# A recurrent attention kernel and its mixing layer: channel tiles in pairs, token weights by hardware loads, another state transpose, a new order

## The chip, the core and the metric

The kernel runs on one core of a Trainium2 chip. The core has five engines with a queue each: TensorE (PE, with its weight loads shown apart as PEld), VectorE (DVE), ScalarE (ACT), GpSimd (POOL) and SyncE (SP). Here SP computes nothing; it issues DMAs. Matrix products go to PSUM, the other data lie in SBUF. The metric is the device time of one execution in microseconds (us). The profile shows one execution; its span runs from the first to the last instruction.

## What is computed

The input has 4 batches, 8 heads, 768 tokens and head width 40, all in fp32. A recurrence over tokens gives `y`, one 40 x 40 state per batch and head, and a mixing layer follows, in which the heads of a token are laid side by side (320 channels):

```python
y[:, :, t] = einsum('bhd,bhde->bhe', r_t, state)
Sa = einsum('bhde,bhe->bhd', state, a_t)
state = state * w_t[:, :, None, :] - einsum('bhd,bhe->bhde', Sa, b_t) + einsum('bhd,bhe->bhde', v_t, k_t)

x = y.transpose(0, 2, 1, 3).reshape(B, S, H * D)
theta = x @ w_theta
yr = einsum('ts,bsd->btd', w_tok_r, x * cos(theta))
yi = einsum('ts,bsd->btd', w_tok_i, x * sin(theta))
u = x + yr + yi
out = u + maximum(u @ w_ch, 0)
```

## The kernel before

The tokens are cut into 24 tiles of 128 (six per batch, numbered 0 to 23 throughout). Within a tile the recurrence is solved with masked matrix products, and the state is carried from tile to tile. The whole program is one list, the string ORDER (L19 to L133). Each entry names a step, a tile, sometimes the engine (A, V and G for ACT, DVE and POOL, S for a DMA transpose issued by SP) and sometimes a PSUM bank (@0 to @3). A loop at L800 calls one function per entry, and `keep` holds the order on every engine. So the place of an entry among those of its own engine is its place in the queue, and a step that waits holds up everything behind it on its engine.

The steps, in the order in which one tile passes through them:

- LDW, LDK, LDB, LDA, LDR, LDV load w, k, b, a, r, v. LDW and LDR load two tiles at once. They go through SP, in four cases at the start through ACT's queue (the letter A).
- LN takes the logarithm of w for two tiles. CSI and CSE are running sums of it by products with triangular masks. INVW and WI are their exponentials. CSE (L384) also makes the sums over a whole tile.
- KH and AH scale k, b and a. TRK and TRA transpose them on PE (eight and four transposes of 128x128), EKBT and EAT copy the results out of PSUM. CV and CR cast v and r, TRV and TRR transpose them, EVT and ERT copy.
- PSI, PHI, LV and LU are score products, eight each, with copies EPSI, EPHI, ELV, ELU. A copy on DVE also masks; a copy on ACT is masked afterwards on POOL (MPSI, MPHI, MLV, MLU).
- X0 and NU (copies ENX, ENU) solve the tile; NUT (copy ENUT) transposes the result. GT makes the new state. The old state is added by a product with the identity (GI) or by an add on DVE (EGA), and EGT scales. GD transposes the state, EGD copies it. Y makes the tile's output, EX scales it into x.
- XT, EXT, TH, ETH and SIN make theta and its sines. ZR multiplies them with x on POOL. LDT loads a row block of a token-weight matrix, WT transposes it, EWT copies it. YR, six entries per tile of two products each, mixes the tokens. EU adds x, UT and EUT transpose u, CH multiplies with w_ch in three products, EO makes the output and ST stores it. LDC loads w_theta and w_ch.

A tile of x or u has 320 channels. It is kept as 384 columns with 64 zeros (`x_t`, `u_t`, L216 and L217), so that transposes (`tr_three`, L646) and products (`mix3`, L660) are three whole ones of 128.

```python
u_t = padded("u", [128, 3 * 128], 3, lambda t: t[:, DM:])
...
wrows[tb, n] = tile_of(wrow, [128, S], BF16, f"wtok_row_{n}")
keep(nc.gpsimd.dma_start(out=wrows[tb, n],
                         in_=moe_w_tok[n][tb * 128:(tb + 1) * 128, :]))
...
tr_one(i, b, "gdps", gt_t[i % 2].rearrange("p g c d -> p (g c) d"))
```

The second piece (L721) is LDT: POOL issues a DMA that turns fp32 into bf16, into one of three buffers per matrix. The third (L615) is GD: four transposes of 128x128 for eight heads of width 40 padded to 64, whose result is bf16.

Of the kernel before, what the change touches and what calls it, by code (L numbers as in the profile page):

```python
# [19 lines left out]
LDW:0 LDK:0A LDB:0 LDA:0A LDA:1 LDB:1A LDK:1 LDV:0A LN:0A LDC:0.0G LDT:0.0G CSI:0@0 LDC:0.1G CSE:0@1 WI:0A  # L20
INVW:0A KH:0V TRK:0@0 AH:0V EKBT:0A TRA:0@3 LDW:2 EAT:0V LDR:0 KH:1V PHI:0@1 PSI:0@0
EPSI:0A MPSI:0G CV:0A LDB:2 EPHI:0A AH:1V TRK:1@1 EKBT:1V LN:2A TRA:1@2 MPHI:0G LDV:1 TRV:0@3
LDK:2 X0:0@0 EAT:1V CSI:2@0 CR:0A ENX:0V LDA:2 PSI:1@1 INVW:2A EVT:0V NU:0 ENU:0A EPSI:1V
TRR:0@1 PHI:1@0 LDB:3 ERT:0A GT:0@2 CV:1A LDK:3 CSE:2@1 EPHI:1V TRV:1@3 ERT:1A NUT:0@0 KH:2G
WI:2A EGT:0V LV:0@0 LDA:3 EVT:1V X0:1@1 ENX:1A ENUT:0A ELV:0V LDV:2 AH:2G GD:0@2 LDR:2 TRK:2@3
KH:3G LV:1@1 NU:1 EKBT:2A LU:0@0 ELV:1V LDW:4 TRA:2@0 ENU:1A LDV:3 ELU:0A NUT:1@3 AH:3G EAT:2V
GT:1@1 ENUT:1V PSI:2@1 TRK:3@0 EGD:0V EPSI:2V LDK:4 LDA:4 GI:1 EKBT:3A CV:2G TRA:3@3 LU:1@0
ELU:1A CR:2G PHI:2@1 EGT:1V X0:2@2 EAT:3V EPHI:2V MLU:0G ENX:2A LN:4A LDB:4 TRR:2@0 PSI:3@0
LDR:4 CV:3G PHI:3@1 MLU:1G Y:0@1 EPSI:3A MPSI:3G EPHI:3V NU:2 TRV:2@3 CSE:4@0 LDV:4 ENU:2A
ERT:2A EVT:2V GT:2@2 EX:0V WI:4A AH:4G CSI:4@1 INVW:4A Y:1@3 LDW:6 NUT:2@1 EGA:2V EGT:2V ERT:3A  # L30
ENUT:2V LV:2@0 LDA:5 TRV:3@2 EX:1V X0:3@1 ELV:2A KH:4G EVT:3V LU:2@1 ENX:3V ELU:2V LV:3@0
TRA:4@0 ELV:3A LDK:5 NU:3 TRK:4@3 LDB:5 GD:1@2 EAT:4V ENU:3A MLV:2G XT:0@0 EKBT:4V CR:4A GT:3@1
GI:3 EGD:1V EGT:3V PSI:4@1 EPSI:4V CV:4G PHI:4@0 LN:6A TRR:4@3 EPHI:4A NUT:3@2 MLV:3G Y:2@1
ENUT:3V LDB:6 LDA:6 AH:5G LDK:6 CSI:6@1 X0:4@2 EX:2V EXT:0A ERT:4A INVW:6A TRV:4@0 ENX:4V
MPHI:4G LDV:5 KH:5G LU:3@0 ERT:5A XT:1@1 NU:4 ELU:3V EXT:1A CSE:6@1 LDV:6 LDT:1.1G ENU:4A
TRA:5@3 WI:6A NUT:4@1 EVT:4V ENUT:4A TRK:5@2 LDK:7 EAT:5V AH:6G XT:2@0 EKBT:5V LV:4@0 TH:0@3
ELV:4V KH:6G PSI:5@1 GD:2@1 LDR:6 SIN:0A TH:1@2 LU:4@0 CV:5G GT:4@3 GI:4 EXT:2A EPSI:5V CV:6G
ZR:0G LDW:8 TRA:6@0 PHI:5@1 LDB:7 ELU:4A LDA:7 EGD:2V EGT:4V TH:2@1 SIN:1A EAT:6V MLU:4G SIN:2A
TRK:6@3 X0:5@0 GD:3@2 EPHI:5V EKBT:6V ENX:5A LDB:8 Y:3@1 ZR:1G EGD:3V EX:3V PSI:6@0 EPSI:6V
TRV:5@3 TRV:6@2 Y:4@1 LN:8A LDK:8 NU:5 PHI:6@1 EVT:6V ENU:5V EVT:5A CR:6G X0:6@2 EPHI:6V  # L40
LDT:1.0G KH:7G TRR:6@0 ENX:6A CSI:8@0 INVW:8A LDA:8 LDV:7 EX:4V NUT:5@3 LV:5@1 ELV:5A LDB:9
ERT:6V AH:7G ENUT:5V TRK:7@1 CSE:8@0 ERT:7V KH:8G TRA:7@3 WI:8A LDV:8 LV:6@1 EAT:7V EKBT:7V
ELV:6A LU:5@0 LDA:9 GD:4@0 NU:6 ELU:5V AH:8G PSI:7@1 TRK:8@3 LDK:9 ENU:6A EGD:4A CV:7A MLV:5G
# [93 lines left out]
def kernel(  # L137
# [247 lines left out]
    def cse(i, b):  # L385
# [448 lines left out]
```

## Time and profile before

| | |
|---|---|
| median of 3 runs | 207.87 us (206.63 to 208.0) |
| the profiled execution | 206.92 us |
| its span | 205.2 us |
| TensorE clock granted, mean | 0.999 |
| DMA | 34.17 MB, mean 167 GB/s |
| chain that ended last | PE 80%, ACT 6%, DVE 5% |

A profile row of instructions gives the line, the engine, the operation, output and inputs by name with their shapes, the count, then busy time and the mean duration in ns. The line is often that of a helper: L270 and L272 are the copies, L275 the multiplication, L278 the product, L282 the transpose. So the names of the tiles tell the steps apart. `sm` and `sc` are small and large PSUM banks. A timeline row gives start and duration in us, and in square brackets how long the engine sat idle before it and on what. Rows marked SPq or ACTq are the DMA issues of a queue.

### The profile page before, as it was taken

To read this page: it belongs to the slowest core of one execution; us is meant where nothing else is said; L and a number is where in the kernel's file an instruction comes from. 1 tells how busy PE (TensorE), PEld (TensorE's weight loads), DVE (VectorE), ACT (ScalarE), POOL (GpSimd) and SP (SyncE) were. 2 spreads that over 40 slices of the span, in tenths; PEclk is the share of its full clock that TensorE was granted. 3 is DMA by queue.
4 is the path that set the end of the run, shared out by engine and by line. 5 is a ranking of instruction groups with operands and counts; after the bars stand their busy time and mean duration, and the time that the engine had idled before them with its cause. 6 is when DMAs were issued, how large, how long until landed. Compare 5 with 4: busy or idle time off the path is not lost.

```text
span 205.2 us, 7809 instructions
## 1 busy us (share of the span) xinstructions
PE 190.1 (93%) x3266; PEld 147.5 (72%) x3266; DVE 170.6 (83%) x334; ACT 154.3 (75%) x259; POOL 147.1 (72%) x157
## 2 busy tenths in 40 slices
PE   0389999999999999999999999999999999999992
PEld 0166777877777887887887877887877787777671
DVE  7256899999999997999799998989888797975653
ACT  2367799997989997999899788987898685822100
POOL 8225778899989699998966886993989785634000
PEclk9999999999999999999999999999999999999999
DMA  7999999998898999899489989987979996433342
GB/s 136 187 240 159 225 171 178 173 230 140 153 221 154 213 159 216 164 213 226 103 171 193 192 172 238 192 135 161 169 97 154 218 129 140 99 90 103 102 150 96
DMA packets 144802, 34.17 MB, mean 167 GB/s; under 512 B 139520, under 2 KB 144768, under 8 KB 144768
## 3 DMA queue, kind: packets, MB, share of 16 engines
q1 hardware_dynamic: 138176, 30.26, 76.5%
q0 software_dynamic: 2432, 2.77, 8.4%
q10 hardware_dynamic: 4160, 0.66, 2.2%
q8 instruction: 25, 0.41, 0.9%
q14 instruction: 9, 0.07, 0.1%
HBM read 29.13 MB, written 3.93 MB: 161 GB/s over the span
## 4 chain that ended last, share of the span: by engine, by line
PE 80%; ACT 6%; DVE 5%; issue 2%; ACTq 2%; POOL 2%; POOLq 0%; DVEq 0%
PE sm L278 39%; PE sc L278 22%; PE sm L282 20%; ACTq L331 1%; ACT kbT L270 1%; ACT psi L270 1%; DVE phi L275 1%; ACTq L326 1%; ACT Wi_two L412 1%; ACT lw_two L338 1%; POOL z L275 1%; DVE lamu L275 1%; DVE rvT L272 1%; POOL lamv L554 1%; POOL phi L554 1%
## 5 line engine op out<-in xcount | busy, mean ns | idle before, releaser
L275 POOL TENSOR_TENSOR kb<-raw_kb,invW_two 128x640 bf16<-128x640 f32 x22 | 33.9, 1542 | 5.5 <-ACT invW_two L373 3.6
L275 POOL TENSOR_TENSOR z<-cs,x 128x640 bf16<-128x640 f32 x22 | 30.8, 1403 | 5.3 <-ACT cs L677 5.3
L278 PE MATMUL sm<-z,wtok_r 128*128 128x320 bf16 x120 | 34.3, 299 | 0.0
L278 PE MATMUL sm<-z,wtok_i 128*128 128x320 bf16 x120 | 34.2, 299 | 0.0
L275 POOL TENSOR_TENSOR ah<-raw_a,Wi_two 128x320 bf16<-128x320 f32 x22 | 19.0, 866 | 8.5 <-issue 5.2
L275 DVE TENSOR_TENSOR psi<-sc,mask_p 128x1024 bf16<-128x1024 f32 x16 | 19.5, 1219 | 1.0 <-PE sc L278 0.9
L554 POOL TENSOR_SCALAR_AFFINE_SELECT psi<-psi 128x1024 bf16<-128x1024 bf16 x8 | 8.7, 1093 | 14.0 <-ACT psi L270 11.6
L275 DVE TENSOR_TENSOR phi<-sc,mask_p 128x1024 bf16<-128x1024 f32 x14 | 17.1, 1219 | 1.6 <-PE sc L278 1.4
L278 PE MATMUL sc<-aT,kbT 64*128 64x128 bf16 x384 | 17.3, 225 | 1.1 <-ACT kbT L270 0.7
L275 DVE TENSOR_TENSOR lamu<-sc,mask_p 128x1024 bf16<-128x1024 f32 x14 | 17.1, 1220 | 0.6 <-PE sc L278 0.3
L282 PE MATMUL sm<-ident,kb 128*128 128x128 bf16 x184 | 14.9, 227 | 2.6 <-DVE kb L275 2.3
L278 PEld LDWEIGHTS <-wtok_r 128*128 128x128 bf16 x144 | 14.0, 97 | 4.6 <-issue 0.3
L270 ACT COPY rvT<-sm 128x512 bf16<-128x512 bf16 x28 | 15.9, 593 | 1.3 <-PE sm L282 0.7
L278 PEld LDWEIGHTS <-wtok_i 128*128 128x128 bf16 x144 | 14.1, 98 | 3.9 <-issue 0.2
L275 DVE TENSOR_TENSOR lamv<-sc,mask_p 128x1024 bf16<-128x1024 f32 x13 | 15.9, 1220 | 1.0 <-PE sc L278 0.5
L677 ACT ACTIVATE cs<-sm 128x320 f32<-128x320 f32 x26 | 9.9, 452 | 8.5 <-PE sm L278 8.4
L278 PEld LDWEIGHTS <-kbT 64*128 64x128 bf16 x384 | 11.9, 97 | 5.8 <-issue 2.4
L278 PEld LDWEIGHTS <-rvT 64*128 64x128 bf16 (+1 forms) x272 | 13.6, 95 | 2.9 <-issue 0.5
L278 PE MATMUL sm<-kb,lamv 128*128 128x40 bf16 x192 | 15.0, 180 | 0.0
L278 PE MATMUL sm<-kb,lamu 128*128 128x40 bf16 x192 | 14.9, 179 | 0.0
L282 PEld LDWEIGHTS <-kb 128*128 128x128 bf16 x184 | 11.5, 101 | 4.2 <-DVE kb L275 2.3
L554 POOL TENSOR_SCALAR_AFFINE_SELECT lamu<-lamu 128x1024 bf16<-128x1024 bf16 x10 | 10.9, 1090 | 4.1 <-ACT lamu L270 4.1
(137 smaller groups left out, 625.0 us busy)
## 6 DMA issues: line engine op xcount, KB each, us to landing
raw_w_two<-in_w_dram SPq DMA_DIRECT2D x12, 320.0 KB, 4.8
raw_r_two<-in_r_dram SPq DMA_DIRECT2D x12, 320.0 KB, 4.8
out_dram<-oo SPq DMA_DIRECT2D x24, 160.0 KB, 2.5
raw_kb<-in_b_dram SPq DMA_DIRECT2D x23, 160.0 KB, 4.6
raw_a<-in_a_dram SPq DMA_DIRECT2D x23, 160.0 KB, 4.5
raw_kb<-in_k_dram SPq DMA_DIRECT2D x23, 160.0 KB, 4.3
raw_v<-in_v_dram SPq DMA_DIRECT2D x23, 160.0 KB, 4.7
wtok_row<-in_moe_w_tok_r_dram POOLq DMA_DIRECT2D x6, 192.0 KB, 4.8
```

The source lines that it names most:

```text
L270: keep(nc.scalar.copy(out=out, in_=in_))
L272: keep(eng[e].tensor_copy(out=out, in_=in_))
L275: keep(eng[e].tensor_tensor(out=out, in0=in0, in1=in1, op=ALU.mult))
L278: keep(nc.tensor.matmul(out, lhsT=lhsT, rhs=rhs, start=start, stop=stop, skip_group_check=True))
L282: keep(nc.tensor.transpose(out=out, in_=in_, identity=ident))
L326: keep(queue[e].dma_start(out=tiles[i].raw_kb[:, j], in_=source(ap, i)))
L331: keep(queue[e].dma_start(out=t, in_=source(ap, i)))
L338: keep(nc.scalar.activation(out=q.lw[:, :, :, 0:D], in_=q.raw_w.rearrange("p h (j d) -> p j h d", j=2), func=AF.Ln))
L412: keep(nc.scalar.activation(out=two, in_=q.cse[:, LO:LO + 2 * DM + 16], func=AF.Exp))
L554: keep(nc.gpsimd.affine_select(out=flat, in_=flat, compare_op=ALU.is_ge, fill=0.0, base=-1, pattern=[[0, 2 * G], [1, 128]], channel_multip ...
L677: keep(nc.scalar.activation(out=cs[i % 5][:, c], in_=tiles[i].theta, func=AF.Sin, bias=(math.pi / 2, 0.0)[c]))
```

## The change

u is kept in pairs of tiles without padding: two tiles side by side are 640 columns, five blocks of 128. The even tile transposes the first two blocks, the odd one the other three. The block in the middle holds the last 64 channels of the even tile and the first 64 of the odd one. The new step CHR multiplies it with two copies of rows of w_ch, each with one half of zeros, for both tiles. So CH takes two products, and CHR one for each of its two tiles. The even tile's output then waits for the odd tile. A step THR would do the same for x, but the new order doesn't use it. w_ch needs four loads in place of two.

The token weights are loaded as fp32 by SP (LDT), into one buffer per matrix, and cast to bf16 by a new step CW, into one buffer per matrix. GD is four products of the state with 80 of the 128 columns of an identity, with a result in fp32. The sums over a tile are a step of their own (CST). No load goes through ACT's queue. The buffers for theta are three, not four. The order is new throughout. Its entries, where the counts differ:

| step | before | after |
|---|---|---|
| GD, GI, EGA | 15, 5, 11 | 16, 9, 7 |
| XT, UT, WT, NUT, TRV | 19, 14, 11, 20, 22 | 16, 16, 12, 22, 23 |
| CH, CHR | 24, 0 | 24, 12 |
| LDT on POOL, on SP | 12, 0 | 0, 12 |
| CW on POOL, on ACT | 0, 0 | 9, 3 |
| LDC | 4 | 6 |
| EGD on DVE, ACT, SP | 7, 8, 5 | 3, 13, 4 |
| EKBT on DVE, ACT | 16, 7 | 20, 3 |
| ENX and ENU on DVE, ACT | 24, 24 | 16, 32 |
| EAT, ERT, EVT, ENUT together on DVE, ACT, SP | 48, 42, 6 | 53, 40, 3 |
| copies of scores on DVE, ACT | 57, 39 | 57, 39 |
| EXT on DVE, ACT, SP | 12, 7, 5 | 11, 5, 8 |
| EUT on DVE, ACT, SP | 6, 8, 10 | 4, 12, 8 |

The diff, cut to its core, with the first and last lines of the order and those around the first token weights:

```diff
-LDW:0 LDK:0A LDB:0 LDA:0A LDA:1 LDB:1A LDK:1 LDV:0A LN:0A LDC:0.0G LDT:0.0G CSI:0@0 LDC:0.1G CSE:0@1 WI:0A
-INVW:0A KH:0V TRK:0@0 AH:0V EKBT:0A TRA:0@3 LDW:2 EAT:0V LDR:0 KH:1V PHI:0@1 PSI:0@0
...
-YR:23.3 YR:23.4 YR:23.5 EU:22V UT:22@1 CH:21@0 EU:23V EUT:22A EO:21V UT:23@3 CH:22@2 EUT:23V
-CH:23@1 EO:22V ST:21 EO:23V ST:22 ST:23
+LDW:2 LDW:0 LDK:0 LDA:1 LDC:0.0G LDC:0.2G LDA:0 LN:0A LDB:0 CSE:0@0 CSI:0@1 LN:2A CST:0 LDB:1
+LDK:1 INVW:0A WI:0A LDK:2 AH:0V CSI:2@1 CSE:2@0 AH:1V KH:0V CST:2 LDB:2 TRA:0@0 TRK:0@3 LDV:0
+EAT:0A INVW:2A LDR:0 EKBT:0V LDA:2 WI:2A KH:1V PHI:0@1 EPHI:0A PSI:0@0 LDV:1 KH:2G TRA:1@2
...
+MPSI:1G GT:0@0 CV:1A EAT:2V EGT:0V ERT:0A NUT:0@2 LDR:2 PSI:2@0 ENUT:0A PHI:2@1 EPSI:2A TRV:1@3
...
+GT:7@0 AH:9G LN:10A TH:3@3 CV:8G LDK:10 EKBT:9V TH:4@1 ELU:7V GI:7 CW:0.0G PHI:8@0 SIN:3A EVT:7V
+LDT:1.0 MLU:6G EGT:7V LV:7@1 SIN:4A TRA:9@2 XT:5@3 EXT:5A X0:8@0 EPHI:8V LDB:10 WT:0.0@1 EAT:9V
+CW:0.1G ENX:8A EWT:0.0A ELV:7V TH:5@3 MLV:6G PSI:9@0 EPSI:9V SIN:5A WT:0.1@2 CR:8G NU:8 TRV:8@1
+EVT:8V LDT:1.1 ENU:8A LDA:10 Y:7@3 EWT:0.1A CV:9G CSI:10@1 EX:7V PHI:9@0 GT:8@0 LDR:10 ZR:5G
+CW:1.0G NUT:8@2 GI:8 LDV:10 EPHI:9V TRR:8@1 EGT:8V Y:6@3 INVW:10A CSE:10@0 KH:10G LDB:11 CST:10
...
+YR:22.5 YR:21.3 EO:19V ST:19 EU:22V YR:21.4 YR:23.0@0 YR:21.5 EU:21V YR:23.1 YR:23.2 YR:23.3
+UT:21@3 YR:23.4 YR:23.5 EU:23V EUT:21A UT:22@1 CH:20@2 EUT:22A CHR:21@3 CH:21 EO:20V UT:23@0
+CH:22@1 EUT:23V ST:20 EO:21V ST:21 CHR:23@2 EO:22V CH:23 ST:22 EO:23V ST:23
...
+    u_two = [consts.tile([128, 2 * DM], BF16, name=f"u_two_{n}") for n in range(3 if twin_u else 0)]
+    def home(i, twins, one, two):
+        if i not in twins:
+            t = one[i % len(one)]
+            return t[:, 0:DM], t
+        t = two[i // 2 % len(two)]
+        if i % 2:
+            return t[:, DM:2 * DM], t[:, 256:2 * DM]
+        return t[:, 0:DM], t[:, 0:256]
...
-    wrow = ctx.enter_context(tc.tile_pool(name="wrow", bufs=3))
+    wraw = ctx.enter_context(tc.tile_pool(name="wraw", bufs=1))
+    wrow = ctx.enter_context(tc.tile_pool(name="wrow", bufs=1))
...
-        tr_one(i, b, "gdps", gt_t[i % 2].rearrange("p g c d -> p (g c) d"))
+        tiles[i].gdps = bank(b)
+        some = ident.rearrange("p (c d) -> p c d", c=2)[:, :, 0:D]
+        for g in range(G):
+            mm(tiles[i].gdps[:, g * 80:g * 80 + 80],
+               gt_t[i % 2][:, g].rearrange("p c d -> p (c d)"), some, True, True)
...
+        elif i % 2 == 0:
+            setattr(q, name, bank(b))
+            for kt in range(2):
+                mm(getattr(q, name)[:, 0:DM], lhs[:, kt, :], rhs[:, kt, :], kt == 0, False)
+        else:
+            for kt in range(2):
+                mm(getattr(q, name)[:, 0:DM], lhs[:, 1 + kt, :], rhs[:, 3 + kt, :], False, kt == 1)
+    def mix_ends(i, b, name, lhs, rhs):
+        setattr(tiles[i], name, bank(b))
+        for c in range(2):
+            mm(getattr(tiles[i - 1 + c], name)[:, 0:DM], lhs[:, 0, :], rhs[:, 2 + 3 * c, :],
+               c == 1, c == 0)
...
-        wrows[tb, n] = tile_of(wrow, [128, S], BF16, f"wtok_row_{n}")
-        keep(nc.gpsimd.dma_start(out=wrows[tb, n],
-                                 in_=moe_w_tok[n][tb * 128:(tb + 1) * 128, :]))
+        wrows[tb, n] = tile_of(wraw, [128, S], FP32, f"wtok_raw_{n}")
+        keep(nc.sync.dma_start(out=wrows[tb, n], in_=moe_w_tok[n][tb * 128:(tb + 1) * 128, :]))
+    def row_cast(tb, n, e):
+        t = tile_of(wrow, [128, S], BF16, f"wtok_row_{n}")
+        copy(e, t, wrows[tb, n])
+        wrows[tb, n] = t
```

330 lines of the change are left out of this document (172 added, 158 removed).

## The prediction

> **What bounds the kernel now.** I read the busy line of the page first, then the windows, to see which engine is full in which stage.
>
> ```profile
> PE 190.1 (93%) x3266; PEld 147.5 (72%) x3266; DVE 170.6 (83%) x334; ACT 154.3 (75%) x259; POOL 147.1 (72%) x157
> ```
>
> The windows give, per stretch: its length, then busy time of PE, of weight loads, of DVE, ACT and POOL, then granted clock, DMA share and GB/s.
>
> ```profile
> 10.00:15.00 5.00, 4.20 (x44) 3.48 (x44) 2.72 (x6) 2.74 (x4) 0.64 (x1) 1.00 1.27 243
> 15.00:20.00 5.00, 4.51 (x59) 3.21 (x57) 3.10 (x5) 4.29 (x8) 3.08 (x3) 1.00 1.13 172
> 20.00:30.00 10.00, 9.38 (x198) 7.22 (x194) 8.78 (x13) 7.92 (x13) 6.98 (x9) 1.00 1.01 197
> 40.00:60.00 20.00, 19.55 (x399) 15.38 (x397) 19.43 (x33) 17.81 (x31) 18.87 (x20) 1.00 0.96 181
> 120.00:140.00 20.00, 20.00 (x373) 16.12 (x371) 18.19 (x31) 17.80 (x32) 16.47 (x16) 1.00 0.91 179
> 190.00:200.00 10.00, 9.96 (x80) 7.05 (x77) 5.86 (x13) 0.76 (x3) 0.00 (x0) 1.00 0.42 129
> ```
>
> There are three regimes. Up to about 20 us there is one dependent chain, and no engine but PE is near full. From 40 to 60 us DVE (19.43 of 20), POOL (18.87) and ACT (17.81) are all nearly full, and PE waits for them in short pieces that its long records hide. From 120 us PE is the bound alone; at 190 ACT has 0.76 of 10 and POOL nothing. So PE work saved is worth its issue time late, and little from 40 to 60, where work saved on DVE or ACT is what counts.
>
> Next the timeline of the start (start, duration, engine).
>
> ```profile
> 0.81 0.46 SPq L320 DMA_DIRECT2D raw_w_two<-in_w_dram  x1
> 1.32 0.57 SPq L326 DMA_DIRECT2D raw_kb<-in_b_dram  x1
> 4.86 1.69 SPq L320 DMA_DIRECT2D raw_w_two<-in_w_dram  x1
> 5.41 0.74 ACT L338 ACTIVATE lw_two<-raw_w_two 128x640 bf16<-128x640 f32 x1 [3.33 <-DMA raw_w_two<-in_w_dram]
> 6.20 0.72 PE L278 MATMUL sc<-lw_two,pair_inc 64*128 64x320 bf16 x4 [6.20 <-ACT lw_two L338]
> 9.17 0.83 DVE L275 TENSOR_TENSOR kb<-raw_kb,invW_two 128x640 bf16<-128x640 f32 x1 [3.76 <-ACT invW_two L373]
> 10.05 1.04 PE L282 MATMUL sm<-ident,kb 128*128 128x128 bf16 x8 [2.26 <-DVE kb L275]
> 10.88 0.63 PE L282 MATMUL sm<-ident,ah 128*128 128x128 bf16 x4
> 12.19 1.03 PE L278 MATMUL sc<-aT,kbT 64*128 64x128 bf16 x16 [0.68 <-ACT kbT L270]
> 19.74 0.71 PE L278 MATMUL sc<-lw_two,pair_exc 64*128 64x320 bf16 x4
> 20.65 0.38 PE L282 MATMUL sm<-ident,v 128*128 128x128 bf16 x4
> ```
>
> LN:0 starts at 5.41; its bracket says that the data came last. PE has its sums of logarithms from 6.20 on and then idles 2.26 us until KH:0 is done, before the first transposes at 10.05. These run at (10.88 - 10.05)/8 = 104 ns each.
>
> PE's price is the distance from start to start, not the recorded duration. Five rows from the middle give it.
>
> ```profile
> 120.71 0.21 PE L278 MATMUL sm<-v,kb 128*128 128x80 bf16 x1
> 121.00 0.57 PE L278 MATMUL sm<-wch,uT 128*128 128x320 bf16 x3
> 121.41 0.20 PE L278 MATMUL sm<-gd,rvT 128*128 128x80 bf16 x1
> 122.66 0.61 PE L282 MATMUL sm<-ident,kb 128*128 128x128 bf16 x8
> 123.11 0.33 PE L282 MATMUL sm<-ident,x 128*128 128x128 bf16 x3
> ```
>
> Eight 80-column products fill 120.71 to 121.00: 36 ns each. Three of 320 columns fill 121.00 to 121.41: 137 ns. Eight transposes fill 122.66 to 123.11: 56 ns.
>
> **The change, part by part.** PE work first, by the order's entries.
> - GD: 15 times four transposes become 16 times four 80-column products: 16 x 4 x 36 - 15 x 4 x 56 = -1.06 us.
> - XT goes from 19 to 16 entries of three transposes: -0.50. UT goes from 14 x 3 = 42 to 41 transposes (two for an even tile, three for an odd one; 16 entries): -0.06. The rest of u and x goes through DMA.
> - WT +1 (six transposes), NUT +2 and TRV +1 (four each): 18 x 56 = +1.01.
> - GI +4 products of 320 columns: +0.55; DVE loses four adds for it.
> - CH and CHR are still 72 products, since the tails were already whole products padded with zeros: 0. CST is only cut out of CSE: 0.
>
> Together -0.06 us: PE, the late bound, gains nothing. I take that figure; both ends are its own terms, -1.6 if only the savings counted late, +1.6 if only the additions did.
>
> Now the other engines.
>
> ```profile
> L723 POOL DMA_DIRECT2D wtok_row<-in_moe_w_tok_r_dram x6 | 3.5, 580 | 0.0
> L272 POOL CAST v<-raw_v 128x320 bf16<-128x320 f32 x15 | 6.8, 453 | 0.1
> L272 POOL CAST r<-raw_r_two 128x640 bf16<-128x640 f32 x7 | 5.0, 720 | 0.0
> L270 ACT CAST r<-raw_r_two 128x640 bf16<-128x640 f32 x5 | 3.6, 729 | 0.0
> L272 DVE COPY kbT<-sm 128x1024 bf16<-128x1024 bf16 x16 | 11.0, 686 | 2.3 <-PE sm L282 2.2
> L373 ACT ACTIVATE invW_two<-sc 128x640 f32<-128x640 f32 x12 | 8.5, 704 | 1.4 <-PE sc L278 1.3
> L272 DVE COPY gd<-sm 128x320 bf16<-128x320 bf16 x7 | 2.2, 318 | 0.4 <-PE sm L282 0.4
> L272 DVE COPY th<-sm 128x320 f32<-128x320 f32 x2 | 1.0, 486 | 0.7 <-PE sm L278 0.7
> L554 POOL TENSOR_SCALAR_AFFINE_SELECT lamv<-lamv 128x1024 bf16<-128x1024 bf16 x11 | 12.1, 1096 | 0.0
> L275 POOL TENSOR_TENSOR z<-cs,x 128x640 bf16<-128x640 f32 x22 | 30.8, 1403 | 5.3 <-ACT cs L677 5.3
> wtok_row<-in_moe_w_tok_r_dram POOLq DMA_DIRECT2D x6, 192.0 KB, 4.8
> DMA to landing us min/median/max: 3.4/4.8/8.6
> ```
>
> - Token weights: POOL loses 12 issues of 0.58 = 7.0 us. It gains nine casts of 128x768, no row of which exists: from 453 and 720 ns at 320 and 640 columns, 720 + 128 x 0.83 = 0.83 us each, 7.5 in all (ends 0.72 and 1.10, the row of a 1024-column pass), and two more weight loads, 1.2 as estimated from the 0.58. POOL +1.7 us, spread over a stage where it has 16.47 of 20; the cover is those 3.5 us of slack per 20, and without it the term is up to +1.7. ACT takes three casts, 3 x 0.85 = 2.6, where it has 17.80 of 20. I take 0 for both.
> - GD's result is now fp32 in PSUM. For DVE that is 486 in place of 318 ns, but DVE keeps three such copies of seven and ACT goes from eight to 13. Hidden: 0. Without cover it is 0.17 on the step from GT to the next Y, three times, +0.5.
> - Copies are dealt out anew: those of scores stay 57 on DVE and 39 on ACT. Of the rest DVE gives up eight negations (ENX, ENU) and the four adds, 12 x 0.49 = 5.9, and takes four copies of kbT, 4 x 0.69 = 2.7, and five more of a, r, v and nu together, at most 0.69 each, 3.4. That is +0.2 of a total of 170.6: 0 for the stretch from 40 to 60, with the ends -3.2 and +0.2.
> - The single raw and single cast buffer per token matrix add waits on SP (LDT behind the previous CW) and on POOL (CW behind LDT's landing). Queued behind them are SP's loads of tiles 10 and 11 and POOL's KH:10. I take 0; the first rival prices it.
>
> The start: all loads now go through SP, and LDW:2 stands ahead of LDW:0. LDW:0 is issued 0.51 later (0.81 to 1.32) and shares its way with a load before it; the ends are 0 (until now it shared its way with ACT's four loads, which are gone) and 1.69 (one full issue, at 4.86). I take 0.6, by the two early rows, where LDW:0 also stands. LN:0 is then at 6.0 and, after 0.74, CSE:0 at 6.75. CSE:0 and CSI:0 take 1.2 (one is recorded with 0.72 and the second overlaps it, an estimate), INVW and WI 0.70 each, AH:0 and AH:1 0.49 each (320 columns), KH:0 0.83: 11.15. Then 1.04 for eight transposes and 0.69 for EKBT, now on DVE: 12.9, less about 0.1 by which records of one engine overlap. PHI:0 is at 12.8 against 12.19: 0.6 late.
>
> Against this stands work done early. Until GT:0 the new order also runs CSE:2 with CST:2 (19.74 to 20.65, 0.91 us), TRK:2 and TRA:2 (12 transposes, 1.25 us at 104 ns), WI:2, EKBT:2, KH:2 and AH:2; CSI:2 falls into the first gap too (0.5). CSI:2, CSE:2 and CST:2 fit into the gap of 2.26 us: 1.4 gained. The 1.25 fit into the 0.80 + 0.49 us that PE has free from 10 to 20 at best. Ends: 0.6 - 1.4 - 1.25 = -2.1, and 1.69 - 1.4 = +0.3. What helps once the copies are the bound (40 to 60) is what DVE and ACT have ahead, EKBT:2 (0.69) and WI:2 (0.70, as INVW), so I take -0.8, between the ends.
>
> The end, from the timeline:
>
> ```profile
> 199.35 0.30 PE L278 MATMUL sm<-z,wtok_i 128*128 128x320 bf16 x1
> 199.69 0.49 DVE L705 TENSOR_TENSOR u<-sm,x 128x320 bf16<-128x320 f32 x1 [0.33 <-PE sm L278]
> 200.43 1.23 PE L278 MATMUL sm<-wch,uT 128*128 128x320 bf16 x6
> 200.67 0.35 DVE L272 COPY uT<-sm 128x384 bf16<-128x384 bf16 x1
> 201.69 0.49 DVE L715 SCALAR_TENSOR_TENSOR oo<-sm,u 128x320 f32<-128x320 f32 x1
> ```
>
> After the last token product (199.35) the new order has two transposes and three pairs of channel products before UT:23, 0.11 + 0.82, so UT:23 at 200.41 and its copy near 200.8 behind EO:20 (0.15 later). Then CHR:23 and CH:23 are four products, and EO:22 waits for CHR:23: 201.2 + 0.27 + 0.17 = 201.65, EO:23 follows at 202.15, against 201.69. I take +0.45; ends +0.15 and +0.7 (one more 0.49 on DVE).
>
> Sum: -0.06 - 0.8 + 0.45 = -0.4 us. The profiled execution took 206.92 us, span 205.2 and 1.72 around it, so 206.5. That execution stands 0.95 us below the median of the runs, 207.87; by the median the sum is 207.5, and I keep the profiled one.
>
> **The rivals.** *Slower: the token weights gate POOL.* LDT:1.0 is issued only when CW:0.0 is through, and CW:1.0 stands right before KH:10 on POOL. Between the two casts lie two selects, a cast of weights, one of r, one of v and a z: 2 x 1.10 + 0.83 + 0.72 + 0.45 + 1.40 = 5.6 us, against 4.8 from issue to landing. If the landing takes more than 5.6, as loads of raw_w_two do (up to 8.6), POOL stands still with KH:10 behind it, and TRK:10 behind that. CW:4.1 to CW:5.1 has the same 5.6. At a landing of 7.2 that is 2 x 1.6 = +3.2, time 209.7; at 8.6 it is +6.0, 212.5. For it speaks that these loads queue behind SP's others; against it the median of 4.8. Chance 0.24, the other ways to end slower with it.
>
> *Faster: PE comes to full rate earlier.* Four transposes are recorded with 0.63 at 10.88 and with 0.38 at 20.65, and eight with 1.04 at 10.05 and 0.61 at 122.66, while the granted clock reads 1.00 in every window. So PE runs at half its rate up to about 20 us. The new opening has CSI:2, CSE:2 and CST:2 in the gap of 2.26 us. If full rate came five microseconds earlier, the 4.51 us of PE from 15 to 20 would take half: -2.2. With the start between -0.8 and its end -2.1 this gives 206.92 - 2.2 - 1.5 + 0.4 = 203.6. Against it: products wait on copies there, so a faster PE may only wait longer. Chance 0.36.
>
> The Trainium skill, page "TensorE: Matmul & The Clock Gate", Part 1, says that the array starts at half rate and is released after about 3.4 us of sustained activity; its 107 and 56 ns agree with the trace's 104 and 56. By that rule alone, with 6.8 as the first product, release would come near 11 and the time near the faster case; but in the kernel before it came some 14 us after the first product (6.20 to 20.65), so the gaps decide.
>
> *The token-weight change does nothing:* 7.0 us of issues replaced by 7.5 of casts is such a case, and is in the forecast.
>
> **How the numbers follow.** About 1% is what a measurement of this kernel can tell from no change. Forecast 206.5, within 1% of 207.87: 0.40, own range 205.5 to 208.5. Faster by over 1% (203.6): 0.36. Slower by over 1% (209.7 and more): 0.24. The range for 8 in 10 runs from 202.5 (the faster case with the start's full -2.1 and 0.5 more) to 210.5 (the slower case at a landing of 7.6).
>
> **What would show it.** LN:0 near 6.0 and PHI:0 near 12.8; CSE:2 before 10; transposes of TRK:2 at 104 or 56 ns; PE busy still full from 120 us; POOL's idle before the casts of token weights under 1 us (right) or some microseconds (the slower rival); EO:23 0.45 later after the last token product than before. Wrong would be a gain or loss of more than a microsecond in the stretch from 40 to 60, where I have put none.

## The result, and the profile after

The changed kernel took 205.49 us (median of 4 runs, 205.31 to 206.6) against 207.94 us for the kernel before beside it. The ratio is 0.9899, with a 95% interval of 0.986 to 0.9938: one per cent faster, a small gain, but the interval ends below 1. In a second set of twelve runs on one chip the ratio was 0.9908 (0.9877 to 0.9938). The profiled execution took 206.6 us with a span of 204.9, so it is the slowest of the four, and 0.3 us below the profiled execution of the kernel before. The ratios here and below leave out executions more than 1.5% above the fastest of their kernel (three of e8's twelve and two of e9's, its profiled one among them).

The page's busy line and the windows of the changed kernel, in the same columns as before:

```profile
PE 187.9 (92%) x3282; PEld 148.3 (72%) x3282; DVE 170.2 (83%) x324; ACT 159.1 (78%) x273; POOL 148.4 (72%) x155
```

```profile
20.00:30.00 10.00, 9.55 (x211) 7.84 (x208) 8.96 (x13) 9.55 (x17) 8.85 (x9) 1.00 0.98 185
30.00:40.00 10.00, 9.79 (x224) 8.26 (x224) 9.57 (x18) 9.09 (x17) 9.32 (x11) 1.00 0.98 188
40.00:60.00 20.00, 19.12 (x397) 15.29 (x395) 19.81 (x35) 19.21 (x32) 19.83 (x21) 1.00 0.98 205
60.00:80.00 20.00, 19.54 (x413) 16.21 (x410) 19.11 (x29) 18.90 (x34) 16.10 (x17) 1.00 0.97 216
80.00:100.00 20.00, 18.75 (x342) 14.87 (x341) 17.58 (x28) 18.34 (x34) 17.50 (x20) 1.00 0.99 198
190.00:200.00 10.00, 9.11 (x74) 6.48 (x73) 6.07 (x13) 1.70 (x4) 0.00 (x0) 1.00 0.40 138
```

Three windows of the kernel before that the prediction didn't show:

```profile
30.00:40.00 10.00, 9.84 (x216) 7.70 (x212) 9.28 (x19) 9.46 (x17) 8.88 (x9) 1.00 1.01 181
60.00:80.00 20.00, 19.70 (x388) 15.50 (x381) 18.70 (x30) 19.47 (x35) 18.20 (x20) 1.00 1.02 184
80.00:100.00 20.00, 20.00 (x385) 16.61 (x383) 17.93 (x30) 18.88 (x33) 18.99 (x22) 1.00 1.03 193
```

Over the four windows from 20 to 80 us DVE, ACT and POOL together were busy for 163.8 us before and 168.3 after (DVE 56.2 and 57.5, ACT 54.7 and 56.8, POOL 52.9 and 54.1). The rise lies mostly in the first two windows: 51.3 and 55.3 us from 20 to 40, then 56.1 and 58.9 from 40 to 60, and 56.4 and 54.1 from 60 to 80. (From 58 us on the casts of the token weights are part of it, which the kernel before doesn't have.) PE's busy time hides what that brings, because a record lasts longer than the distance to the next start (19.55 before and 19.12 after from 40 to 60, with 399 and 397 products). So I counted another way: each product that has not yet started at a time is priced by start-to-start distances, much as in the prediction (56 ns a transpose, 136 for 320 columns, 35 for 80, 25.5 for 40, 32 a score product, 83 a sum of logarithms). The table gives how much less PE work is left than in the kernel before, in us. The last two columns are the price of all PE work and the start of the last product:

```text
kernel                 20 us  40 us  80 us  100 us  160 us  180 us  195 us   all     last
before                  0      0      0      0       0       0       0      168.5   201.4
changed                 1.05   2.03   2.73   1.07    2.02    1.26    0.33   168.5   201.0
changed, again (e12)    1.17   2.20   2.22   0.42    1.27    1.20    0.06   168.5   201.8
e2_gd_transposes       -0.08   1.15   2.36   1.72    2.64    2.61    0.74   169.8   200.5
e3_soft_loads           0.72   1.63   2.01   1.23    1.33    1.26    0.33   168.5   201.0
e5_order_alone_six     -0.72   0.45   1.59   0.87    1.30    1.14    0.27   170.1   200.9
e6_single_u_six         0.61   1.64   2.51   1.70    2.62    2.47    1.77   168.8   199.4
e7_old_order_new_start  0.47   0.00  -0.39  -0.60   -0.30   -0.95   -1.50   168.5   202.8
e8_early_weights        1.05   2.03   2.71   0.42    1.22    1.14    0.19   168.5   201.1
e10_end_mended          0.72   1.63   2.52   1.56    2.39    2.31    2.37   168.5   198.9
e11_end_mended_single   0.90   1.87   2.29   0.54    1.55    1.34    1.36   168.8   199.8
```

The changed kernel is 2.7 us ahead at 80 us: 1.05 of that is there at 20 us, 1.0 comes from 20 to 40, 0.2 from 40 to 60 (counted the same way, the lead at 60 is 2.2) and 0.5 from 60 to 80. It loses 1.7 by 100 us, 0.7 from 170 to 180, and 1.0 from 190 to 195. What is left at the end is 0.3. The table compares single executions, and that of the kernel before was 0.95 us below the median of its runs, while those of the changed kernel were the slowest of four and of twelve; so it tells in which stretch work is gained or lost, and its last columns are not the times.

**The start.** The timeline of the changed kernel:

```profile
5.36 1.36 ACT L361 ACTIVATE lw_two<-raw_w_two 128x640 bf16<-128x640 f32 x2 [3.28 <-DMA raw_w_two<-in_w_dram]
6.14 0.72 PE L301 MATMUL sc<-lw_two,pair_exc 64*128 64x320 bf16 x4 [6.14 <-ACT lw_two L361]
8.87 0.89 DVE L298 TENSOR_TENSOR ah<-raw_a,Wi_two 128x320 bf16<-128x320 f32 x2 [3.42 <-DMA raw_a<-in_a_dram]
10.11 0.83 DVE L298 TENSOR_TENSOR kb<-raw_kb,invW_two 128x640 bf16<-128x640 f32 x1 [0.34 <-DMA raw_kb<-in_b_dram]
10.99 1.04 PE L305 MATMUL sm<-ident,kb 128*128 128x128 bf16 x8 [0.70 <-DVE kb L298]
12.81 1.03 PE L301 MATMUL sc<-aT,kbT 64*128 64x128 bf16 x16 [0.79 <-DVE kbT L295]
17.44 0.61 PE L305 MATMUL sm<-ident,v 128*128 128x128 bf16 x4
17.84 1.06 PE L305 MATMUL sm<-ident,r 128*128 128x128 bf16 x8
19.00 0.41 PE L305 MATMUL sm<-ident,ah 128*128 128x128 bf16 x4
19.70 0.20 PE L301 MATMUL sm<-v,kb 128*128 128x80 bf16 x1 [0.28 <-ACT nu L547]
```

LN:0 starts at 5.36, not later than before (5.41), though LDW:0 now stands second. AH:0 and AH:1 start at 8.87; the bracket names LDA:0, which is fifth on SP, but WI:0 on ACT (8.03 to 8.74) was not through much sooner. What holds the chain of tile 0 is the row below: KH:0, now behind both, waits another 0.34 us for LDB:0, sixth on SP, and PHI:0 starts at 12.81. In the second profile of the changed kernel (e12) these loads land about a microsecond later, and PHI:0 starts at 13.84:

```profile
10.00 0.89 DVE L298 TENSOR_TENSOR ah<-raw_a,Wi_two 128x320 bf16<-128x320 f32 x2 [4.55 <-DMA raw_a<-in_a_dram]
11.13 0.83 DVE L298 TENSOR_TENSOR kb<-raw_kb,invW_two 128x640 bf16<-128x640 f32 x1 [0.24 <-DMA raw_kb<-in_b_dram]
17.44 0.62 PE L301 MATMUL sc<-aT,kbT 64*128 64x128 bf16 x16
```

In the first profile the four transposes at 17.44 are recorded with 0.61, the eight at 17.84 with 1.06 (half rate, up to 18.70) and the four at 19.00 with 0.41: full rate comes about 1.6 us earlier than before, where it came between 19.74 and 20.65. In e12 it is there by 17.44, where sixteen score products are recorded with 0.62 for the 1.03 at 12.81. GT:0 starts at 19.70; in the kernel before, where its first product of that name is the row below, it was 0.61 us earlier, with less work done.

```profile
19.09 0.25 PE L278 MATMUL sm<-v,kb 128*128 128x80 bf16 x1
```

**The loss at 92 us.** The chain that ended last, the timeline of ACT and POOL, and a window:

```profile
86.97 5.88 DMA wtok_raw<-in_moe_w_tok_i_dram
```

```profile
92.87 0.83 ACT L293 CAST wtok_row<-wtok_raw 128x768 bf16<-128x768 f32 x1 [1.33 <-DMA wtok_raw<-in_moe_w_tok_i_dram]
93.46 1.54 POOL L298 TENSOR_TENSOR kb<-raw_kb,invW_two 128x640 bf16<-128x640 f32 x1 [1.45 <-PE sm L301]
```

```profile
92.00:94.00 2.00, 1.27 (x20) 1.08 (x20) 2.00 (x4) 1.13 (x2) 0.55 (x2) 1.00 0.88 142
```

LDT:3.1 lands 5.88 us after its issue. CW:3.1 on ACT waits for it 1.33 us with EVT:12 and WI:14 queued behind, and PE is busy for only 1.27 of these 2 us.

**The losses at 171 and 192 us:**

```profile
170.68 0.86 POOL L298 TENSOR_TENSOR ah<-raw_a,Wi_two 128x320 bf16<-128x320 f32 x1 [1.34 <-DMA raw_a<-in_a_dram]
191.56 0.30 PE L301 MATMUL sc<-z,wtok_i 128*128 128x320 bf16 x1
191.90 0.49 DVE L751 TENSOR_TENSOR u_two<-sc,x_two 128x320 bf16<-128x320 f32 x1
192.44 0.30 PE L301 MATMUL sc<-z,wtok_r 128*128 128x320 bf16 x1 [0.58 <-DVE u_two L751]
194.82 0.30 PE L301 MATMUL sc<-z,wtok_r 128*128 128x320 bf16 x1 [0.31 <-DVE u_two L751]
198.65 0.30 PE L301 MATMUL sm<-z,wtok_i 128*128 128x320 bf16 x1
```

AH:23 waits for LDA:23. Later PE waits twice for an add EU: two tiles of the last batch share one PSUM tile, EU:18 reads one half of it, and YR:19.5, which writes the other half, stands right behind EU:18 in both orders. In the old order PE has YR:20.2 and YR:20.3, four products, to do between YR:18.5, the last that EU:18 needs, and YR:19.5. In the new order it has YR:19.4 alone, into the same PSUM tile: EU:18 starts at 191.90, when these products are through, and YR:19.5 at 192.44, when EU:18 is.

### The profile page after: what moved, and what is told of

The parts are those of the page before. It is cut to its first block, busy times and chain, and to the rows that moved or that the text cites. A ratio compares the mean times of both kernels' runs of the same rounds, so it can differ in the third digit from the quotient of the medians.

```text
span 204.9 us, 7844 instructions
## 1 busy us (share of the span) xinstructions
PE 187.9 (92%) x3282; PEld 148.3 (72%) x3282; DVE 170.2 (83%) x324; ACT 159.1 (78%) x273; POOL 148.4 (72%) x155
## 4 chain that ended last, share of the span: by engine, by line
PE 61%; ACT 16%; DMA 10%; DVE 6%; SPq 3%; issue 2%; POOL 0%; DVEq 0%; ACTq 0%; POOLq 0%
PE sm L301 31%; PE sc L301 15%; PE sm L305 14%; DMA wtok_raw<-in_moe_w_tok_i_dram 3%; DMA raw_v<-in_v_dram 3%; DMA raw_kb<-in_b_dram 2%; DMA raw_a<-in_a_dram 2%; ACT cs L723 2%; ACT rvT L293 2%; DVE rvT L295 1%; ACT L723 1%; ACT L321 1%; SPq L349 1%; SPq L354 1%; ACT psi L293 1%
## 5 line engine op out<-in xcount | busy, mean ns | idle before, releaser
L298 POOL TENSOR_TENSOR z<-cs,x_two 128x640 bf16<-128x640 f32 x22 | 30.7, 1401 | 6.4 <-ACT cs L723 5.6
L298 DVE TENSOR_TENSOR phi<-sc,mask_p 128x1024 bf16<-128x1024 f32 x17 | 20.7, 1220 | 2.6 <-PE sc L301 2.5
L298 DVE TENSOR_TENSOR psi<-sc,mask_p 128x1024 bf16<-128x1024 f32 x15 | 18.3, 1217 | 0.6 <-PE sc L301 0.5
L295 DVE COPY kbT<-sm 128x1024 bf16<-128x1024 bf16 x20 | 13.7, 686 | 2.2 <-PE sm L305 2.1
L293 ACT COPY rvT<-sm 128x512 bf16<-128x512 bf16 x24 | 14.0, 594 | 1.5 <-PE sm L305 1.3
L580 POOL TENSOR_SCALAR_AFFINE_SELECT lamv<-lamv 128x1024 bf16<-128x1024 bf16 x13 | 14.2, 1094 | 1.2 <-ACT lamv L293 1.1
L298 DVE TENSOR_TENSOR lamv<-sc,mask_p 128x1024 bf16<-128x1024 f32 x11 | 13.4, 1220 | 0.5 <-PE sc L301 0.4
L293 ACT CAST lamv<-sc 128x1024 bf16<-128x1024 f32 x13 | 13.2, 1013 | 0.8 <-PE sc L301 0.5
L301 PEld LDWEIGHTS <-lamv 128*128 128x128 bf16 x192 | 13.3, 96 | 0.5
```

The costliest lines, as they stand in the source:

```text
L293: keep(nc.scalar.copy(out=out, in_=in_))
L295: keep(eng[e].tensor_copy(out=out, in_=in_))
L298: keep(eng[e].tensor_tensor(out=out, in0=in0, in1=in1, op=ALU.mult))
L301: keep(nc.tensor.matmul(out, lhsT=lhsT, rhs=rhs, start=start, stop=stop, skip_group_check=True))
L580: keep(nc.gpsimd.affine_select(out=flat, in_=flat, compare_op=ALU.is_ge, fill=0.0, base=-1, pattern=[[0, 2 * G], [1, 128]], channel_multip ...
```

## The experiments

All ratios are to the kernel before, run beside each on the same chip, with a 95% interval; the kernels of one call share those runs.

### The order alone, and each part undone

e1 and e5 have the new order and all three parts undone. The edits, on the changed kernel:

```diff
 GD:
-        for g in range(G):
-            mm(tiles[i].gdps[:, g * 80:g * 80 + 80], gt_t[i % 2][:, g]..., some, True, True)
+        tr_one(i, b, "gdps", gt_t[i % 2].rearrange("p g c d -> p (g c) d"))
 LDT (the CW entries go):
-        keep(nc.sync.dma_start(out=wrows[tb, n], in_=moe_w_tok[n][tb * 128:(tb + 1) * 128, :]))
+        keep(nc.gpsimd.dma_start(out=wrows[tb, n], in_=moe_w_tok[n][tb * 128:(tb + 1) * 128, :]))
 u (CHR goes, CH is three products again):
-CHR:1@2 CH:1
+CH:1@2
-    u_t = padded("u", [128, 3 * 128], min(3, B * NCH - len(twin_u)), lambda t: t[:, DM:])
+    u_t = padded("u", [128, 3 * 128], 6, lambda t: t[:, DM:])
```

e1 and e4 kept three tiles for u. The new order writes tiles in another sequence, so EO there adds the u of a later tile in some places; with six tiles (e5, e6) it doesn't.

> The new order with all three parts undone: GD as four transposes, token weights by POOL's converting DMA without casts, u in single padded tiles. My theory: the gain of the changed kernel (0.990 of the time before) comes from the order, above all from tile 2's sums, transposes and scaling done in the opening, and the parts cancel. Then this stays faster than before: ratio 0.988 to 0.996. Rival: the parts bring the gain (80-column products, hardware loads) and the order alone is worth nothing: ratio 0.998 to 1.010.

> The new order with all three parts undone, and six single tiles of u in place of three (with three, the new order overwrites a tile of u that is still to be read, and an add waits for it). My theory: the order carries most of the gain, the parts cancel up to the 80-column products (worth 0.5%): ratio to before 0.990 to 0.996. Rival: the order alone gives nothing, 0.998 to 1.005.

e1 gave 0.995 (0.9921 to 0.9979), e5 0.9901 (0.9865 to 0.9938). With none of the three parts, the new order is as fast as the changed kernel (0.9899 and 0.9908). The rival falls: the order carries the gain, and the three parts together add nothing that can be measured (the intervals reach some 0.8 us to either side). The table says it too: e5 begins with 1.6 us more PE work (170.1 for 168.5), stands 0.97 behind at 15 us, and is 1.59 ahead at 80.

> The changed kernel with GD as four transposes again. PE has 16 x 4 x (56 - 36) = 1.28 us more work. My theory: PE is the bound only from about 100 us on, where two thirds of the GD entries stand, so 0.6 to 1.3 us slower than the changed kernel: ratio to before 0.993 to 0.997. Rival: the fp32 result makes the copy on DVE slower (486 for 318 ns) and the step lies on the chain, so undoing it costs nothing or gains: 0.987 to 0.990.

e2 gave 0.9955 (0.9921 to 0.999). That is half a per cent above the changed kernel, about 1.1 us, as the 1.28 us of PE work would have it, but the intervals overlap, and e5, which has the same transposes, shows no such loss. Undoing it is not a gain, so the rival falls; the size stays open.

> The changed kernel with the token weights loaded by POOL's converting DMA again, three buffers, no casts. ACT loses 3 casts of 0.83 and the wait of 1.33 us before one of them, POOL loses nine casts of 0.83 and gains 12 issues of 0.58. My theory: casts and issues are hidden, only the wait at 91.5 to 92.9 us counts, so 0.5 to 1.5 us faster than the changed kernel: ratio to before 0.983 to 0.988. Rival: the converting DMA is itself a cost (POOL's issues come back between its scaling steps, and its queue is slower): 0.990 to 1.000.

e3 gave 0.9897 (0.9862 to 0.9932): the same as the changed kernel. Taking away all twelve casts and the wait at 92 us gained nothing. My range of 0.983 to 0.988 failed, and the other side's began at 0.990. By the table its lead at 100 us is 1.23 against the changed kernel's 1.07; counted the same way at 120 us, which is no column of the table, it is 0.72 against 1.43.

> The changed kernel with u in single padded tiles again: 16 x 3 = 48 transposes in place of 41 (+0.4 us of PE), the same 72 products, no wait of an even tile for its odd one, and a shorter end (0.45 us by my reckoning). My theory: the two cancel, within 0.4 us of the changed kernel: ratio to before 0.988 to 0.992. Rival: the wait for the odd tile held PSUM banks and output, so undoing it is worth a microsecond or more: below 0.985.

> The changed kernel with u in six single padded tiles. 7 more transposes (+0.4 us of PE), no wait of an even tile for its odd one, an end that is shorter by 0.45 us. My theory: within 0.4 us of the changed kernel, ratio to before 0.988 to 0.992. Rival: pairing is worth half a per cent or more by itself: 0.995 to 1.000.

e4 gave 0.9938 (0.9915 to 0.9961), e6 0.993 (0.9895 to 0.9965), both a little above the 0.992 at which my range ended, and the intervals overlap with those of the pairs. One profile of e6 shows a better end (last product at 199.4 us), but the median of its timed runs shows no gain; a lead in one profile is not a time.

### The opening on the old order

The kernel before, with this opening; the six entries are taken out of their old places:

```diff
-LDW:0 LDK:0A LDB:0 LDA:0A LDA:1 LDB:1A LDK:1 LDV:0A LN:0A LDC:0.0G LDT:0.0G CSI:0@0 LDC:0.1G CSE:0@1 WI:0A
-INVW:0A KH:0V TRK:0@0 AH:0V EKBT:0A TRA:0@3 LDW:2 EAT:0V
+LDW:0 LDW:2 LDK:0 LDB:0 LDA:0 LDA:1 LDB:1 LDK:1 LDV:0 LN:0A LDC:0.0G LDT:0.0G CSI:0@0 LDC:0.1G CSE:0@1 LN:2A
+WI:0A INVW:0A CSI:2@0 CSE:2@1 KH:0V TRK:0@0 AH:0V EKBT:0A TRA:0@3 INVW:2A WI:2A EAT:0V
```

> The kernel before with the new opening alone: all loads on SP, LDW:2 second, and LN:2, CSI:2, CSE:2, INVW:2, WI:2 done before the first score products; everything from KH:2 on as before. My theory: the lead that the new order has at 10 us (1.2 us of PE work by issue distances) is kept through the stretch in which the copies are the bound only as far as ACT is ahead by INVW:2 and WI:2 (1.4 us): 0.5 to 1.2 us faster than before, ratio 0.994 to 0.998. Rival: the opening is given back within 20 us, since the chain of tile 0 is what counts there and it starts later: 0.999 to 1.003.

It is slower: 1.0046 (1.0015 to 1.0076). Its timeline:

```profile
4.15 0.74 ACT L334 ACTIVATE lw_two<-raw_w_two 128x640 bf16<-128x640 f32 x1 [2.07 <-DMA raw_w_two<-in_w_dram]
4.94 0.72 PE L274 MATMUL sc<-lw_two,pair_inc 64*128 64x320 bf16 x4 [4.94 <-ACT lw_two L334]
12.70 1.03 PE L274 MATMUL sc<-aT,kbT 64*128 64x128 bf16 x16 [1.89 <-ACT Wi_two L408]
22.05 0.92 PE L278 MATMUL sm<-ident,kb 128*128 128x128 bf16 x8
23.87 0.40 PE L278 MATMUL sm<-ident,ah 128*128 128x128 bf16 x4
```

and the last DMA issue of ACT in the kernel before:

```profile
3.65 1.71 ACTq L331 DMA_DIRECT2D raw_v<-in_v_dram  x1
```

The sums of logarithms start at 4.94 in place of 6.20, for two reasons. Before, the data of LDW:0 landed 4.0 us after their issue at 0.81, at 4.8, but ACT was issuing its fourth DMA until 5.36, and LN:0 started at 5.41, though its bracket names the data. In e7 ACT issues nothing, and the same load lands sooner, 3.3 us after its issue, so LN:0 starts at 4.15. Still PHI:0 comes at 12.70, later than before, since it now waits for WI:2 on ACT. The lead of 1.3 us at 10 us is 0.47 at 20 and -0.13 at 25. The last part goes with PE's rate: the eight transposes at 22.05 are still recorded with 0.92, and the four at 23.87 with 0.40, so full rate comes near 22.7 (by the distances between single products), two microseconds later than before. So this opening by itself is not the gain; but with PHI:0 behind WI:2, which the new order avoids, and with full rate so late, it doesn't tell what work done early is worth. (This opening isn't the new one entry by entry, and KH:2 and TRK:2 stayed in their old places, so the new opening with its own continuation isn't judged by it.)

### The new order for the first 70 us, the old one after

```diff
+(436 entries of the new order, up to YR:0.0, without CST, CW and CHR; ACT does EVT:9 and ENU:9)
+EVT:9A NU:9 EKBT:10A ELU:8V ENU:9A
+LDW:12 LDT:2.1G LDA:11 WT:1.1@1 EWT:1.1V ... (the old order's entries that are left)
```

> The kernel before with the new order's entries up to its first YR (436 entries, about the first 70 us), then the old order's for all that is left; the old forms of GD, token loads and u throughout. My theory: the gain is made before that point, by DVE, ACT and POOL being kept fuller from 20 to 80 us; it shows as a lead of 1.0 to 2.7 us of PE work over the kernel before by 90 us, and the old remainder keeps it, since there PE is full: ratio to before 0.987 to 0.995. Rival: the gain of the new order lies in its later part (or is given back at the seam): lead under 0.5 at 100 us, ratio 0.998 to 1.005.

It is slower, 1.0067 (1.0033 to 1.0101), and does not answer the question, as the seam breaks. Its profile is of the slowest of twelve executions (211.63 us, mean granted clock 0.983). Of the other eleven nine have a mean clock of 0.988 to 0.992, so they lost clock too, though less; the one at 1.0 took 207.26 us, a little less than the kernel before (207.75). The windows from 70 us and two rows of PE:

```profile
70.00:72.00 2.00, 1.13 (x18) 0.77 (x17) 2.00 (x3) 1.16 (x2) 1.83 (x2) 1.00 1.22 238
72.00:74.00 2.00, 0.31 (x4) 0.29 (x4) 1.26 (x2) 1.22 (x2) 2.00 (x3) 0.73 1.17 207
74.00:76.00 2.00, 2.00 (x28) 1.61 (x26) 0.45 (x2) 0.45 (x1) 1.15 (x2) 0.50 0.81 109
76.00:78.00 2.00, 2.00 (x22) 1.80 (x22) 1.23 (x2) 1.20 (x3) 1.37 (x2) 0.50 1.23 234
78.00:80.00 2.00, 2.00 (x42) 1.35 (x39) 1.55 (x3) 1.97 (x4) 1.85 (x2) 0.56 0.95 177
```

```profile
73.72 0.82 PE L278 MATMUL sm<-ident,wtok_row 128*128 128x128 bf16 x6 [1.69 <-DMA wtok_row<-in_moe_w_tok_i_dram]
75.87 1.03 PE L278 MATMUL sm<-ident,kb 128*128 128x128 bf16 x8
```

A row block that the old order would have loaded earlier isn't there, PE waits 1.69 us for it, and in that wait the granted clock falls to 0.50 and stays there until nearly 80 us. A mean of 0.73 from 72 to 74 means 1.08 us at 0.50, so it fell at about 72.9: some seven microseconds at half rate. By the count of the table it is 1.41 us ahead at 70 us and 3.02 behind at 80; from there to 160 it stays within 0.5 of that. So the old remainder neither gains nor loses for 80 us, as the theory had it (it loses another 1.5 from 160 to 180), but that the lead of the first 70 us would be kept to the end is not shown.

### Two mends

e8 moves two loads of the changed kernel forward, e10 moves three entries, e11 is e10 with u in six single tiles:

```diff
 e8
-LDV:12 LDA:13 LDR:12 LDB:14 LDT:3.1
+LDT:3.1 LDV:12 LDA:13 LDR:12 LDB:14
 e8, e10, e11
-LDB:23 LDK:23 LDA:23
+LDA:23 LDB:23 LDK:23
 e10, e11
-EU:18V YR:19.5
+YR:19.5 EU:18V
-EU:20V EUT:19A CH:18@3 YR:21.2
+YR:21.2 EU:20V EUT:19A CH:18@3
```

> The changed kernel with LDT:3.1 issued six loads earlier on SP (before LDV:12) and LDA:23 two earlier, nothing else. In the changed kernel's profile ACT sits idle 1.33 us for the landing of LDT:3.1 and PE has 1.27 of 2 us busy there; POOL sits idle 1.34 us for LDA:23 and PE loses 0.54. My theory: both gaps are on the path, 0.8 to 1.8 us faster than the changed kernel, ratio to before 0.981 to 0.986. Rival: the waits are made good afterwards by the copies' slack, or the landing waits for other loads instead: 0.988 to 0.992.

e8 gave 0.9922 (0.989 to 0.9955): no gain. The row block is there in time, but the loads behind it are not. The list of waits from 82 to 102 us has, in place of ACT's wait:

```profile
POOL v L292 <- DMA raw_v<-in_v_dram: 1.5, 1, 1.5
PE sm L302 <- POOL ah L295: 1.0, 1, 1.0
```

It loses 2.3 us from 80 to 100 us, more than the changed kernel (1.7). The loads stand in one queue, SP's, and moving one forward moved the wait to the next.

> The changed kernel with three entries moved: YR:19.5 ahead of EU:18, YR:21.2 ahead of EU:20 (PE waited 0.58 and 0.31 us for these two adds, which read the other half of the PSUM tile that PE writes next), and LDA:23 two loads earlier (PE lost 0.5 us at 171). My theory: at the end nothing makes up for a wait of PE, so 0.7 to 1.4 us faster than the changed kernel run beside it: ratio to before 0.983 to 0.987. Rival: the adds come later and the last outputs with them, nothing gained: within 0.3 us of it.

> The changed kernel itself, beside the three others on one chip. Both theories: ratio to before 0.986 to 0.994, as measured. It tells how far one profile's waits for loads (1.33 us for a row block of token weights, 1.34 for LDA:23) come back in another: if they are the order's, both are there again within 0.5 us; if they are chance, they are not.

e10 gave 0.9825 (0.9789 to 0.986), 204.29 us, its runs between 203.98 and 204.76. The changed kernel beside it gave 0.9908, 205.76 us, runs from 204.9 to 207.37. The intervals don't touch: with pairs the three moved entries are worth 1.5 us, and this version beats both kernels. The list of PE's waits from 188 to 198 us is empty for e10, and in its timeline the products run on where the wait of 0.58 was (0.34 us from start to start, for 0.88 from 191.56 to 192.44):

```profile
191.25 0.30 PE L298 MATMUL sc<-z,wtok_i 128*128 128x320 bf16 x1
191.59 0.29 PE L302 MATMUL sm<-ident,u_two 128*128 128x128 bf16 x2
```

The lead at 195 us is 2.37, against 0.33 and 0.06 in the two profiles of the changed kernel. How much of it is LDA:23 wasn't tried by itself: the second profile of the changed kernel loses nothing from 170 to 180, so that wait comes and goes, while both waits for EU come back there:

```profile
PE sc L301 <- DVE u_two L751: 0.9, 2, 0.6
```

The wait for token weights comes back on ACT in e12, 1.1 us for 1.3, and in e11, 0.9, each with 1.8 us lost from 80 to 100. But in e10, which has the same entries there, no cast waits for its load, nor does one on ACT in e2 and e6; these three lose 0.6 to 1.0. So the order allows this wait, and whether it comes differs from one execution to the next.

> As the run before, with u in six single tiles. By PE's lead over the kernel before, single tiles stood 0.7 us better than pairs at 195 us, in one profile. My theory: pairs save 0.4 us of transposes and cost 0.45 at the end, so within 0.4 us of the run with pairs: 0.982 to 0.988. Rival: the pairs are a loss, 0.980 or below.

e11 gave 0.99 (0.9853 to 0.9947), above the 0.988 at which my range ended. Beside e10 the pairs are not a loss, so the rival falls; whether they are a gain is open, as the intervals just overlap. The same waits are gone, but its lead at 100 us was only 0.54 in this profile. With single tiles the three moved entries are not a measured gain: e6, without them, gave 0.993 (0.9895 to 0.9965).

## Why the prediction came out as it did

The forecast was 206.5 us, within 1%, from a sum of -0.4 us. Measured is 205.49, inside the range and 0.01 below its own narrower one, on the border between no change and faster. The direction was right, and the sum too small by about 1 us against the profiled run and 1.7 by the ratio. Between the two profiled executions the difference is 0.3 us, close to the forecast, but by luck: the one before lies 0.95 us below the median of its runs, the one after 1.1 above.

- *PE's work, -0.06.* Right: by the products of the two traces it is 168.5 us in both (at the same prices, so this confirms the counts).
- *POOL's and ACT's casts, 0.* Right: without them (e3) the time is the same. The cast on POOL took 0.83 us, as estimated.
- *The start, -0.8.* The size is near the mark (the lead at 20 us is 1.05, in e12 1.17) and PHI:0 came at 12.81 for 12.8, but that is luck, as the way was another. LN:0 started at 5.36 and not near 6.0: its load, now second, landed 1.2 us later than the one that stands first in e7, but the loads on ACT's queue had cost LN:0 as much before (5.41 for 4.15). About half of the 0.6 us so saved was lost where KH:0 waits for LDB:0, for which the sum has no wait; in e12 that load came a microsecond later, and PHI:0 at 13.84. And the lead isn't only work done early (EKBT:2, WI:2), as the term has it. A part is the earlier full rate. Counted from 15 to 20 us the lead grows by 0.8 to 0.9 in the profiles where full rate came between 17.2 and 17.7 (e1, e4, e12), by 0.6 where it came between 18.0 and 18.4 (e2, e8, e9, e11) and by 0.2 to 0.3 where it came at 18.9 to 19.1 (changed, e3, e5, e6, e10).
- *The stretch from 40 to 60 us, 0.* This held: the lead went from 2.03 to 2.2 us there (in e12 from 2.20 to 1.8), so the sign of being wrong that I had named did not come. The step that failed is another: the sum has no term for the stretches around it. From 20 to 40 us the lead grew by 0.9 to 1.2 in all nine profiles of the table that have the new order, from 60 to 80 by 0.4 to 0.8. From 20 to 40 this goes with the copying engines, which had room before: busy for 51.3 us of 60, and for 55.3 in the changed kernel. From 60 to 80 it doesn't (56.4 before, 54.1 after), and its cause stays open. A count of entries over the whole kernel can't see either. The count itself was near the mark (DVE 170.6 us before and 170.2 after, for +0.2), though it left out seven copies of EGD, EUT and EXT that DVE gives up and two that it takes. e5 has the same growth with the old forms of everything, so it is the order; which entries of it do it stays open, since e9 broke at its seam.
- *The slower rival.* Its mechanism was there, in another place: the gate was CW:3.1 on ACT and not a cast on POOL, with a landing of 5.88 us against the 5.6 that I gave as the point from which it decides (worked out for POOL, so the nearness is chance). With that wait the lead falls by 1.7 to 1.8 us from 80 to 100 us, without it by 0.6 to 1.0 (e2, e3, e6, e10); but as e3 and e8 show, it takes the place of other waits, and in the timed runs its absence was worth nothing that could be measured.
- *The faster rival.* Right in kind, but too large. Full rate came 1.6 us earlier in the profiled execution, and 1.6 to 3.4 in all profiles with the new order, not five, and it goes with the 0.2 to 0.9 us of lead above, not with 2.2. Only one profile of the kernel before was taken, so how much its own point (20.65) varies is not shown. By the rule of the Trainium skill, page "TensorE: Matmul & The Clock Gate", Part 1 (half rate until about 3.4 us of sustained activity), it would have come near 10, an estimate from the first product at 6.14. Measured is between 18.7 and 19.1, 12 us or more after the first product, so in this opening that rule doesn't give the time. That the gaps between the products are the reason is likely, but not tested.
- *The end, +0.45.* From the last token product to the start of the last EO it took 2.34 us before (199.35 to 201.69). After, the last EO started at 201.32 by the chain's row below, so 2.67: +0.33, close. Not seen was what stood just before, the two waits for EU, 0.89 us; the order's text showed them (YR:19.4 alone between YR:18.5 and YR:19.5, with EU:18 before the last), and I had read only its last three lines.

```profile
201.32 0.49 DVE oo L760
```

## What to carry to other kernels

Where several engines share the work, a count of instructions over the whole kernel says nothing of what a new order brings: follow the work that is left on the bounding engine over time, in both kernels and in more than one execution of each. A lead made early is only worth what later waits leave of it, and waits near the end, where nothing can make up for them, are the cheapest to mend. When two results share one PSUM tile, put the last product into the second half ahead of the read of the first.

## What the runs showed that I had not expected

- In both kernels the granted clock reads 1.00 in the windows up to 20 us, while products run at half rate (four transposes recorded with 0.61 us at 17.44, 0.41 at 19.00). In e9 the same row does show it: 0.50 from 74 to 78 us, with eight transposes recorded with 1.03 as at the start. So at the start that row can't be relied on; the distance of the products can. When full rate comes differs by almost two microseconds among profiles with the same opening (by 17.44 in e12, near 19.1 in the changed kernel), and the lead gained from 15 to 20 us follows it.
- In e9 the clock fell at about 72.9 us. PE had been busy for 1.13 us of 70 to 72 and then idle since 72.03 (73.72 less 1.69), so for 0.9 us, and some seven microseconds at half rate followed. The Trainium skill, page "TensorE: Matmul & The Clock Gate", Part 1, puts the return to half rate at an idle window of about 3.4 us; here a thinly filled stretch was enough.
- The wait that a bracket names need not be the one that counts: before, LN:0's named its data, which were there at 4.8, while ACT's fourth DMA issue held it until 5.36. Nor is the wait with the longest bracket the one on the path: AH:0's 3.42 us for LDA:0 ended with WI:0, and KH:0's 0.34 for LDB:0 came on top.
